# Stage 1 of batches 3 and 4: exponentials, sums and holds in other slots, and the first hi matmul one slot earlier

## The chip, the cores and the metric

The kernel runs on one core of a Trainium2 chip. The metric is the device time of one execution in microseconds (us), as the median of three runs. A core has five engines with an instruction queue each: TensorE (PE in the profile; its weight loads are PEld), VectorE (DVE), ScalarE (ACT), GpSimd (POOL) and SyncE (SP, which issues most DMA transfers here). An engine takes its instructions in order; where one needs another engine's result, it waits for a semaphore, and what is queued behind it waits too. [...]

## The reference, cut to what matters

```python
def mab(q, kv):
    s = scale * (q @ kv.transpose(0, 2, 1))
    s = s - s.max(-1, keepdims=True)
    a = np.exp(s)
    a /= a.sum(-1, keepdims=True) + 1e-09
    return a @ kv

h = mab(I, x)                 # stage 1: 32 learned rows over all 12416 rows of a batch
y = mab(x, h)                 # stage 2: each row of x over the 32 rows of h

gate = 1.0 / (1.0 + np.exp(-(y @ w_gate)))
val = y @ w_val
out = (gate * val @ w_out).astype(np.float32)
```

x has 4 batches of 12416 rows of 128 columns; the gated feed-forward network has 1536 hidden columns.

## The kernel before

**Blocks, steps and slots.** The feed-forward network runs over 97 blocks of 512 rows (24 for each batch and one of the remaining rows). Stage 2's last product is folded into the network: the attention weights `a2r` are multiplied with `hw`, which is h times the network's weights. A block is eight steps, by turns one with two hidden tiles (1024 columns, wide) and one with one (512, narrow). A step is: value matmul into `v_ps`, tanh of the gate on ScalarE (line 971, `t`), the product `u = (t + 1) * v` on VectorE (line 984), and, two steps later, its projection into the accumulator `acc_ps` on TensorE (line 1015). The gate matmul `g_ps` runs two steps ahead. Value and gate banks of each width are single, and so is the accumulator: ScalarE empties it once a block (line 1033, `o`), and the next block's first projection waits for that.

**The order by hand.** Two steps are a slot, a wide product and a narrow one. All work beside the network (stages 1 and 2 of later groups and batches) is written into a table: `at(slot, make, late)` puts a piece at a slot, early behind the wide step or late behind the narrow one. `beside` issues the pieces when their step comes, so the table sets each engine's order. The row tiles of a batch go in groups of 16 (`groups`), six full ones and a small one of one tile, number NG. While the network works on batch b (slots `o` to `o + 95`, with `o = 96 b`, b from 0), stage 1 of batch b + 1 is in the table, and slots given below as plain numbers count from `o`; slots from 100 on count from the start.

**Stage 1.** For a recent group `plan_stage1` puts down: scores on TensorE and their maximum on VectorE (`begin`, lines 217 and 229), the exponential on ScalarE with the negated maximum as its bias (`weigh`, line 242), a transpose by DMA on SP's queue (`turn`, line 266), the sums over x on TensorE in two halves (line 277) and a copy of the sum out of PSUM (`s1_sum_keep`, line 292, `hst`). In batches 3 and 4 (b = 1 and 2 in the loop) this is done for groups 2, 3 and NG alone, with scores at slots 7, 11 and 32. The four older groups, `SHARED`, go by `plan_shared`: their scores are copied to SBUF (line 337), share one maximum that GpSimd works out, and are weighed later (line 374). They are summed in pairs: two groups into one bank, `hp`, and one copy (`hold`, line 386) for each pair. Scores, sums and several other small results use the one PSUM bank with the tag "m", each after the one before has been read. The kept sums are joined at slot 54 (`plan_combine`, `join`).

**Stage 2's first whole group.** The group right after the start is done with `soon`: its maximum is split on GpSimd into two bf16 parts, `hi` and `lo` (lines 546 and 548), which two matmuls with an identity add onto the scores in PSUM (`s2_shift`, line 555); the exponential reads PSUM after that.

## Time and profile before

| | |
|---|---|
| median of 3 runs | 722.02 us (721.89 to 722.83) |
| the profiled execution: its time | 722.04 us |
| the profiled execution: its span, first to last instruction | 720.2 us |
| mean granted TensorE clock | 1.000 of full speed |
| VectorE busy in the span | 97% |
| ScalarE busy | 94% |
| TensorE busy (matmuls are pipelined, so this is not TensorE at its peak) | 90% |
| GpSimd busy | 61% |

In a row of the timeline the first number is the start in us from the span's start, the second the time to the end of the row's last instruction; then come the engine (SPq is SP's DMA queue), the line, the operation, the tiles as out<-in, the shape of the row's first instruction (later ones in the row may have another), and the count. In brackets stand idle time ahead of the row and what ended it. `a1T` and `a1` of the code are `a1T` and `a`, `o32` is `o`, `s1_ps` and `s2_ps` are `s_ps`.

### The profile page before, as it was taken

How to read it: one execution, taken by the hardware profiler on the slowest of the kernel's cores; microseconds unless marked ns; L12 is line 12 of the kernel's file. 1: busy time of each engine (PE TensorE's matmuls, PEld its weight loads, DVE VectorE, ACT ScalarE, POOL GpSimd, SP SyncE). 2: the span in 40 equal slices, each digit the busy share in tenths (PEclk: the TensorE clock that was granted, in tenths of full speed). 3: DMA queues.
4: the chain of work that ended last, by engine and by line, in shares of the span. 5: the costliest groups of instructions: out<-in, count | busy, mean ns of one | idle time of the engine just before them, and what ended most of it. 6: DMA issues, size and time to landing. Idle time of an engine off the chain costs nothing.

```text
span 720.2 us, 21611 instructions
## 1 busy us (share of the span) xinstructions
PE 647.8 (90%) x8478; PEld 392.9 (55%) x8478; DVE 700.7 (97%) x865; ACT 675.0 (94%) x1012; POOL 437.6 (61%) x739
## 2 busy tenths in 40 slices
PE   7989889998998999999998989999989899898887
PEld 4555555555555555655555555555555555555555
DVE  4799999999999999999999999999999999999998
ACT  4699999999999999999999999999999999999996
POOL 4464663877558988558657897486746555535100
PEclk9999999999999999999999999999999999999999
DMA  8879935263593255155485132220232123121211
GB/s 171 171 140 177 180 80 106 74 119 83 112 160 77 65 103 114 52 125 112 90 140 118 55 75 62 59 76 33 74 74 60 46 63 70 47 61 45 62 45 46
DMA packets 116726, 65.21 MB, mean 91 GB/s; under 512 B 99824, under 2 KB 101008, under 8 KB 116624
## 3 DMA queue, kind: packets, MB, share of 16 engines
q1 hardware_dynamic: 111936, 49.81, 31.2%
q0 software_dynamic: 4416, 13.90, 10.8%
q8 instruction: 66, 1.08, 0.6%
q14 instruction: 36, 0.29, 0.2%
q10 hardware_dynamic: 272, 0.13, 0.1%
HBM read 27.80 MB, written 25.43 MB: 74 GB/s over the span
## 4 chain that ended last, share of the span: by engine, by line
DVE 52%; issue 22%; PE 14%; ACT 8%; DMA 2%; DVEq 1%; POOL 0%; ACTq 0%; POOLq 0%
DVE u L984 50%; ACT t L971 7%; PE acc_ps L1015 7%; PE v_ps L952 5%; DMA xn<-in_x_dram 2%; DVEq L984 1%; PE hp_ps L277 1%; DVE nm L229 1%; ACT o L1033 1%; PE g_ps L952 1%; PE s_ps L217 0%; POOL xn L82 0%; ACT a1T L242 0%; ACT hwt L434 0%; ACT sc L565 0%
## 5 line engine op out<-in xcount | busy, mean ns | idle before, releaser
L984 DVE SCALAR_TENSOR_TENSOR u<-t,v_ps 128x512 f16<-128x512 f16 (+1 forms) x778 | 676.1, 942 | 2.7 <-PE g_ps L952 1.4
L971 ACT ACTIVATE t<-g_ps 128x512 f16<-128x512 f32 (+1 forms) x777 | 593.0, 819 | 25.4 <-ACT t L971 13.0
L952 PE MATMUL v_ps<-a2r,hwt 32*128 32x512 f16 (+1 forms) x1188 | 293.5, 371 | 59.6 <-DVE u L984 57.2
L1015 PE MATMUL acc_ps<-wo,u 128*128 128x128 f16 x4656 | 327.4, 220 | 1.5 <-ACT o L1033 1.2
L1015 PEld LDWEIGHTS <-u 128*128 128x128 f16 x4656 | 261.5, 98 | 89.3 <-issue 88.3
L952 PE MATMUL g_ps<-a2r,hwt 32*128 32x512 f16 (+1 forms) x1188 | 296.6, 377 | 0.0
L952 PEld LDWEIGHTS <-hwt 32*128 32x128 f16 x2424 | 92.4, 91 | 192.8 <-issue 147.0
L645 POOL TENSOR_TENSOR a2n<-e,rs 128x2048 f16<-128x2048 f16 (+3 forms) x25 | 86.8, 3474 | 5.3 <-DVE rs L617 3.6
L599 POOL TENSOR_TENSOR sum<-e 128x256 f32<-128x256 f16 (+1 forms) x23 | 15.4, 672 | 116.1 <-ACT e L591 116.1
L623 POOL TENSOR_TENSOR near<-sme,minus 128x16 f32<-128x16 f32 (+1 forms) x22 | 65.2, 2961 | 1.7
L1033 ACT ACTIVATE o<-acc_ps 128x512 f32<-128x512 f32 x96 | 58.2, 606 | 0.0
L575 POOL TENSOR_TENSOR rise<-sc 128x256 f32<-128x256 f32 (+1 forms) x22 | 16.3, 739 | 40.7 <-ACT sc L565 40.6
L576 POOL TENSOR_SCALAR rise<-rise 128x256 f32<-128x256 f32 (+6 forms) x110 | 30.1, 273 | 9.7
L579 POOL TENSOR_TENSOR top<-top,rise 128x128 f32<-128x128 f32 (+3 forms) x88 | 28.3, 322 | 7.3
L599 POOL TENSOR_TENSOR sum<-sum 128x128 f32<-128x128 f32 (+3 forms) x92 | 28.3, 307 | 7.2
L575 POOL TENSOR_TENSOR rise<-top 128x128 f32<-128x128 f32 (+3 forms) x88 | 27.2, 309 | 6.9
L582 POOL TENSOR_TENSOR sc<-sc,top 128x512 f32<-128x512 f32 (+1 forms) x22 | 23.9, 1086 | 1.7
L531 PEld LDWEIGHTS <-xT 128*128 128x128 f16 x388 | 13.0, 96 | 11.5 <-issue 11.1
L82 POOL DMA_DIRECT2D xn<-in_x_dram x25 | 14.7, 595 | 6.5 <-DMA xn<-in_x_dram 5.6
L531 PE MATMUL s_ps<-hT,xT 128*128 128x32 f16 x388 | 18.0, 178 | 0.1
L579 POOL TENSOR_TENSOR top<-sc,rise 128x256 f32<-128x256 f32 (+1 forms) x22 | 16.2, 738 | 1.8
L362 POOL TENSOR_SCALAR xT<-xT,nm 128x512 f32<-128x512 f32 x8 | 15.8, 1990 | 0.2
(141 smaller groups left out, 271.3 us busy)
## 6 DMA issues: line engine op xcount, KB each, us to landing
out_dram<-o SPq DMA_DIRECT2D x96, 256.0 KB, 2.3
xn<-in_x_dram POOLq DMA_DIRECT2D x19, 512.0 KB, 7.4
xn<-in_x_dram POOLq DMA_DIRECT2D x4, 544.0 KB, 6.3
a2r<-a2n SPq DMA_TRANSPOSE x29, 4.5
xn<-in_x_dram POOLq DMA_DIRECT2D x1, 384.0 KB, 14.9
wg<-in_moe_w_gate_dram POOLq DMA_DIRECT2D x1, 384.0 KB, 16.4
wv<-in_moe_w_val_dram POOLq DMA_DIRECT2D x1, 384.0 KB, 16.4
wo<-in_moe_w_out_dram POOLq DMA_DIRECT2D x1, 384.0 KB, 15.9
```

Of the source, the lines that this page charges most:

```text
L531: nc.tensor.matmul(s2[:, j, :], xT[b][:, c + j, :], hT16[b][:], start=(j == 0), stop=whole and j == j1 - 1, skip_group_check=True,)
L575: nc.gpsimd.tensor_tensor(out=r, in0=far, in1=near, op=ALU.subtract)
L576: nc.gpsimd.tensor_scalar(out=r, in0=r, scalar1=BIG, scalar2=0.0, op0=ALU.min, op1=ALU.max)
L579: nc.gpsimd.tensor_tensor(out=top[:, 0:n, 0:w], in0=near, in1=r, op=ALU.add)
L599: nc.gpsimd.tensor_tensor(out=d[:, 0:n, :], in0=src[:, :, 0:w], in1=src[:, :, w : 2 * w], op=ALU.add)
L623: nc.gpsimd.tensor_tensor(out=near[:, 0:n], in0=sme[:, 0:n], in1=minus1[:, 0:n], op=ALU.pow)
L645: eng.tensor_tensor(out=a2n[:, 0:n, :, :], in0=e.unsqueeze(2).to_broadcast((P, n, 4, m)), in1=rs.unsqueeze(2).unsqueeze(3).to_broadcast((P ...
L952: st[what + "end"] = nc.tensor.matmul(pt[:, k, col : col + nb * P], hw[b][r : r + 32, j // 2, :], a2r[r : r + 32, o : o + nb, :].rearrange ...
L971: st["tanh"] = nc.scalar.activation(out=st["t"][:, :, c:e], in_=st["g"][:, :, c:e], func=AF.Tanh, scale=0.5)
L984: u = nc.vector.scalar_tensor_tensor(out=st["u"][:, :, c:e], in0=st["t"][:, :, c:e], scalar=1.0, in1=st["v"][:, :, c:e], op0=ALU.add, op1= ...
L1015: nc.tensor.matmul(acc[0][(i // 2) % len(acc[0])][:, i, :], st["u"][:, k, ts(i, P)], wo16[:, NI * (j % 2) + j // 2, :], start=(j == 0 and ...
L1033: nc.scalar.mul(out=o32[:], in_=acc[0][0][:], mul=0.5)
```

## The change

Five edits, four of them in batches 3 and 4:

- the exponentials of groups 2 and 3 stand in the slot of their maximum, late, and not in the next one; their DMA turns follow one slot sooner too;
- each of the four shared sums is issued in two halves, in two slots running; the second pair starts at slots 49 and 51, before 50 and 52;
- the copy of the first pair's sum moves from slot 43 to 45 (the second stays at 53);
- the sum of the small group and its copy move from slot 45 to 47;
- in stage 2's `soon` group the hi matmul is issued in slot 2, the lo matmul stays in slot 3.

No operation is added or taken away, and each engine has as many instructions as before.

```diff
@@ plan_stage1
         at(score, begin)
-        at(score + 1, weigh, late=full)
-        at(score + 2, turn)
+        soon = full and b > 1
+        at(score + (0 if soon else 1), weigh, late=full)
+        at(score + (1 if soon else 2), turn)
@@ plan_shared
-        def part(i):
-            if i % 2 == 0:
+        def part(i, k0, k1):
+            if i % 2 == 0 and k0 == 0:
                 st["hp"] = ps.tile([P, C + 1], F32, tag="m", name="hp_ps")
-            s1_sum_pe(b, SHARED[i], st[i], st["hp"], 0, 4, i % 2 == 0, i % 2 == 1)
+            s1_sum_pe(b, SHARED[i], st[i], st["hp"], k0, k1, i % 2 == 0, i % 2 == 1)
...
-            at(o + sums[i], lambda i=i: part(i))
+            at(o + sums[i], lambda i=i: part(i, 0, 2))
+            at(o + sums[i] + 1, lambda i=i: part(i, 2, 4))
...
-        for k in range(2):
-            at(o + sums[2 * k + 1] + 1, lambda k=k: hold(k))
+        for k, slot in enumerate(holds):
+            at(o + slot, lambda k=k: hold(k))
@@ plan_stage2
         if soon:
-            at(weigh, lambda: s2_shift(GC, st["s2"], *st["hl"]))
+            for k in range(2):
+                at(weigh - 1 + k, lambda k=k: s2_shift(GC, st["s2"], *st["hl"], which=(k,)))
@@ the table of slots
-        single = (32, (45, 45, 45) if b else (43, 43, 43))
+        single = (32, (47, 47, 47) if b else (43, 43, 43))
...
-                b + 1, o, (-6, 2, 10, 14), (7, 11, 15), 23, (26, 30, 42, 46), (40, 42, 50, 52)
+                (26, 30, 42, 46),
+                (40, 42, 49, 51),
+                (45, 53),
```

(`s2_shift` takes the list `which` and issues only the named ones of its two matmuls.)

Three places show how the queues change. The first is ScalarE's queue around slot 103 (7 from batch 2's start), where batch 3's first recent group is weighed; `t` is the network's tanh, `a1T` the exponential, `o` the accumulator's copy. Before:

```order
L971 ACTIVATE t_4680<-g_ps 128x1024
L971 ACTIVATE t_4697<-g_ps 128x512
L971 ACTIVATE t_4719<-g_ps 128x1024
L971 ACTIVATE t_4728<-g_ps 128x512
L242 ACTIVATE a1T<-s_ps,nm_0_137 128x512
L1033 ACTIVATE o_4744<-acc_ps 128x512
L971 ACTIVATE t_4755<-g_ps 128x1024
```

and after:

```order
L974 ACTIVATE t_4680<-g_ps 128x1024
L974 ACTIVATE t_4697<-g_ps 128x512
L242 ACTIVATE a1T<-s_ps,nm_0_137 128x512
L974 ACTIVATE t_4721<-g_ps 128x1024
L974 ACTIVATE t_4732<-g_ps 128x512
L1036 ACTIVATE o_4746<-acc_ps 128x512
L974 ACTIVATE t_4757<-g_ps 128x1024
```

The exponential passes two tanhs and no longer stands directly ahead of the accumulator's copy.

The second is SP's DMA queue in the same place; `a<-a1T` is the turn of the weighed group, `xT<-xn` a transpose of x for a later score. Before:

```order
L656 DMA_TRANSPOSE a2r<-a2n 128x16x128
L91 DMA_TRANSPOSE xT_3912<-xn_1800 128x16x128
L1035 DMA out_dram<-o_4744 128x512
L266 DMA_TRANSPOSE a_4757<-a1T 128x4x128
L1035 DMA out_dram<-o_4887 128x512
```

and after:

```order
L658 DMA_TRANSPOSE a2r<-a2n 128x16x128
L266 DMA_TRANSPOSE a_4723<-a1T 128x4x128
L91 DMA_TRANSPOSE xT_3912<-xn_1800 128x16x128
L1038 DMA out_dram<-o_4746 128x512
L266 DMA_TRANSPOSE a_4867<-a1T 128x4x128
```

The turn, which needs the exponential, now stands ahead of the transpose of x and of an output store.

The third is TensorE's queue at slots 2 and 3, where the `soon` group is shifted; `g_ps` and `v_ps` are gate and value fills. Before:

```order
L952 MATMUL g_ps<-a2r,hwt 128x512
L555 LDWEIGHTS identb
L555 MATMUL s_ps<-hi,identb 128x512
L555 LDWEIGHTS identb
L555 MATMUL s_ps<-lo,identb 128x512
L952 LDWEIGHTS hwt
L952 MATMUL v_ps<-a2first,hwt 128x256
```

and after, where hi now stands:

```order
L955 MATMUL g_ps<-a2first,hwt 128x256
L557 LDWEIGHTS identb
L557 MATMUL s_ps<-hi,identb 128x512
L955 LDWEIGHTS hwt
L955 MATMUL v_ps<-a2first,hwt 128x256
```

hi now precedes a narrow step's value fills in slot 2; lo keeps its place alone.

More of the change, by code (lines that the diff above doesn't have):

```diff
@@ L322, in plan_stage1, with plan_shared @@
         at(keep, lambda: s1_sum_keep(b, s, st["hp"]))
-    def plan_shared(b, o, takes, tops, least, weighs, sums):
+    def plan_shared(b, o, takes, tops, least, weighs, sums, holds):
         st = {}
@@ L551, in s2_max, with s2_shift @@
         return hi, lo
-    def s2_shift(n, s2, hi, lo):
-        for t_, last in ((hi, False), (lo, True)):
+    def s2_shift(n, s2, hi, lo, which=(0, 1)):
+        for t_, last in [((hi, False), (lo, True))[k] for k in which]:
             nc.tensor.matmul(
@@ L1065 @@
             plan_shared(
-                b + 1, o, (-6, 2, 10, 14), (7, 11, 15), 23, (26, 30, 42, 46), (40, 42, 50, 52)
+                b + 1,
+                o,
+                (-6, 2, 10, 14),
+                (7, 11, 15),
+                23,
+                (26, 30, 42, 46),
+                (40, 42, 49, 51),
+                (45, 53),
             )
```

## The prediction, made before the result was known

> **What bounds the kernel now.** I read the page's busy table first, then its costliest groups, then the timelines of VectorE, ScalarE and TensorE stretch by stretch. From the page:

> ```profile
> span 720.2 us, 21611 instructions
> PE 647.8 (90%) x8478; PEld 392.9 (55%) x8478; DVE 700.7 (97%) x865; ACT 675.0 (94%) x1012; POOL 437.6 (61%) x739
> L984 DVE SCALAR_TENSOR_TENSOR u<-t,v_ps 128x512 f16<-128x512 f16 (+1 forms) x778 | 676.1, 942 | 2.7 <-PE g_ps L952 1.4
> ```

> The gated products of line 984 fill the span: VectorE waits only 2.7 us ahead of them. So the time is what the products take back to back, plus other VectorE work, plus what makes a product late. ScalarE at 94% and TensorE at 90% have little room, so work that lands badly on either delays VectorE. The sum is made against this execution's 722.04 us, which encloses the 720.2 us span and is as good as the median of the runs, 722.02. The measure of "late" is an undisturbed stretch, VectorE's timeline in the last batch (start, length, first shape, count):

> ```profile
> 551.38 42.71 DVE L984 SCALAR_TENSOR_TENSOR u<-t,v_ps 128x1024 f16<-128x1024 f16 x49
> ```

> 49 products, starting and ending with a wide one, are 24 slots and a last product of 1.21: a slot is (42.71 - 1.21) / 24 = 1.729 us. The same timeline where batch 3's stage 1 runs, and batch 4's:

> ```profile
> 215.04 1.21 DVE L984 SCALAR_TENSOR_TENSOR u<-t,v_ps 128x1024 f16<-128x1024 f16 x1
> 216.17 0.68 DVE L229 TENSOR_REDUCE nm<-s_ps 128x1 f32<-128x512 f32 x1
> 216.77 4.13 DVE L984 SCALAR_TENSOR_TENSOR u<-t,v_ps 128x512 f16<-128x512 f16 x5
> 221.28 2.99 DVE L984 SCALAR_TENSOR_TENSOR u<-t,v_ps 128x1024 f16<-128x1024 f16 x3 [0.37 <-PE g_ps L952]
> 224.18 0.68 DVE L229 TENSOR_REDUCE nm<-s_ps 128x1 f32<-128x512 f32 x1
> 229.27 2.99 DVE L984 SCALAR_TENSOR_TENSOR u<-t,v_ps 128x1024 f16<-128x1024 f16 x3 [0.35 <-PE g_ps L952]
> ...
> 385.96 0.68 DVE L229 TENSOR_REDUCE nm<-s_ps 128x1 f32<-128x512 f32 x1
> 391.07 2.99 DVE L984 SCALAR_TENSOR_TENSOR u<-t,v_ps 128x1024 f16<-128x1024 f16 x3 [0.37 <-PE g_ps L952]
> 393.97 0.68 DVE L229 TENSOR_REDUCE nm<-s_ps 128x1 f32<-128x512 f32 x1
> 399.06 15.14 DVE L984 SCALAR_TENSOR_TENSOR u<-t,v_ps 128x1024 f16<-128x1024 f16 x17 [0.35 <-PE g_ps L952]
> ```

> The two maxima of a batch lie four slots apart. Undisturbed that would be 4 x 1.729 plus the maximum's own 0.60 (216.17 to 216.77), 7.52 us; measured are 224.18 - 216.17 = 8.01 and 393.97 - 385.96 = 8.01. Each first exponential thus costs 0.49 us. The second has nearly the same idle gap (0.35 for 0.37), so I take 0.48. Over both batches 1.94 us.

> **Part 1: the four exponentials, one slot sooner.** ScalarE's timeline says what makes them costly (an idle mark tells of the time before the row's first instruction); the last three rows are an undisturbed slot with an output copy, two of ScalarE and VectorE's product:

> ```profile
> 217.31 1.51 ACT L971 ACTIVATE t<-g_ps 128x1024 f16<-128x1024 f32 x2 [0.54 <-PE g_ps L952]
> 218.70 0.69 ACT L242 ACTIVATE a1T<-s_ps,nm 128x512 f16<-128x512 f32 x1
> 219.27 0.61 ACT L1033 ACTIVATE o<-acc_ps 128x512 f32<-128x512 f32 x1
> ...
> 255.20 0.61 ACT L1033 ACTIVATE o<-acc_ps 128x512 f32<-128x512 f32 x1
> 255.67 1.53 ACT L971 ACTIVATE t<-g_ps 128x1024 f16<-128x1024 f32 x2
> 255.49 1.21 DVE L984 SCALAR_TENSOR_TENSOR u<-t,v_ps 128x1024 f16<-128x1024 f16 x1
> ```

> and on TensorE:

> ```profile
> 219.93 0.83 PE L1015 MATMUL acc_ps<-wo,u 128*128 128x128 f16 x12 [0.31 <-ACT o L1033]
> ...
> 255.95 0.84 PE L1015 MATMUL acc_ps<-wo,u 128*128 128x128 f16 x12
> ```

> The exponential (218.70) stands directly ahead of the copy that empties the accumulator. The copy comes late, the projection waits 0.31 us for its one bank, the value and gate fills queue behind the projection, and the product at 221.28 is late. Two slots earlier ScalarE sat idle for 0.54 us ahead of 217.31, because the maximum on VectorE had stretched that slot. The exponential moves there.

> It cannot start before the maximum ends, 216.17 + 0.68 = 216.85; with about 0.06 for the signal (an estimate: the copy ends at 219.27 + 0.61 = 219.88 and the projection that it lets go starts at 219.93) it starts at 216.91. It holds ScalarE 0.57 (218.70 to 219.27), so the next tanh starts near 217.48, not 217.31. That tanh is due only at 216.77 + 0.60 + 1.73 = 219.10, when its product is: hidden. The copy follows the two tanhs. From 217.31 to 218.70, where the exponential stood, is 1.39, so the copy starts at 217.48 + 1.39 = 218.87 and the next tanh at 219.35, 0.25 behind the slot's first product at 219.10. In the undisturbed slot it starts 255.67 - 255.49 = 0.18 behind, so copy and tanh come some 0.07 later than normal. In that slot the projection (255.95 above) starts 0.09 after the copy's signal (255.20 + 0.61 + 0.05 = 255.86), so nearly all of this is swallowed; I leave 0.03 for each exponential. Of the 0.49, idle time is 0.37, the overlap of neighbouring products that a gap also loses 0.08 (216.17 + 0.68 against 216.77), and the other 0.04 belongs to the shared score's copy in the next slot, of which I leave 0.03. Gain of part 1: 1.94 - 4 x 0.06 = **1.70 us**. Bounds: the old gaps stay (0), or all goes (1.94); I stay near the upper one because the idle 0.54 us is measured in the very place.

> [...]

> With each exponential its DMA turn moves on SP's queue, ahead of the last full transpose of x (SP's queue in the timeline, then two rows of the list of DMA issues, whose last number is the median time to landing):

> ```profile
> 214.52 2.54 SPq L91 DMA_TRANSPOSE xT<-xn  x1
> 220.29 1.21 SPq L266 DMA_TRANSPOSE a<-a1T  x1
> ...
> xT<-xn SPq DMA_TRANSPOSE x21, 4.7
> a<-a1T SPq DMA_TRANSPOSE x18, 3.2
> ```

> That transpose of x was issued at 214.52; now it stands behind a turn that waits for the exponential, 216.91 + 0.69 = 217.60, and issues for 1.21, so it starts at about 218.85 and lands near 223.6 by the median of 4.7. The first who needs it is the last shared score, in slot 14 beside the product at 229.27. Covered by over 5 us: nothing. The output store behind it goes later; nobody waits for it, with four output buffers. The turn's own result is used six slots on or more.

> **Part 2: shared sums over two slots each.** VectorE in windows of nine products, with a whole sum in each second slot, then with halves in each slot (the recent groups' sums) and with none:

> ```profile
> 274.19 7.79 DVE L984 SCALAR_TENSOR_TENSOR u<-t,v_ps 128x512 f16<-128x512 f16 x9
> 291.95 7.81 DVE L984 SCALAR_TENSOR_TENSOR u<-t,v_ps 128x512 f16<-128x512 f16 x9
> 444.27 7.79 DVE L984 SCALAR_TENSOR_TENSOR u<-t,v_ps 128x512 f16<-128x512 f16 x9
> 461.82 7.82 DVE L984 SCALAR_TENSOR_TENSOR u<-t,v_ps 128x512 f16<-128x512 f16 x9
> 232.18 7.60 DVE L984 SCALAR_TENSOR_TENSOR u<-t,v_ps 128x512 f16<-128x512 f16 x9
> 246.25 7.59 DVE L984 SCALAR_TENSOR_TENSOR u<-t,v_ps 128x512 f16<-128x512 f16 x9
> ```

> A pair of whole sums costs 0.20, 0.22, 0.20 and 0.23 over 7.59; halves cost 0.01 for four of them. So 0.85 - 4 x 0.01 = **0.81 us**, between 0.43 (if a half cost half a whole) and 0.85. The second pair is summed a slot sooner; a turn lands 3.2 us after issue (median) and the last has four slots, 6.9 us.

> **Part 3: holds.** The first hold moves from slot 43 to 45 and the small group's from 45 to 47, each one copy of about 0.28 us. Other such copies stand in slots 17 and 19, within the 7.60 row, so the new places cost nothing. Their bank is asked for again at slots 47 and 49, after the copies. If that cover went, it would be 0.1 to 0.2 us each.

> **Part 4: first hi matmul.** VectorE, GpSimd, then TensorE around slots 2 and 3:

> ```profile
> 35.43 6.65 DVE L984 SCALAR_TENSOR_TENSOR u<-t,v_ps 128x1024 f16<-128x1024 f16 x7
> 34.97 0.20 POOL L546 CAST hi<-nmx 128x16 bf16<-128x16 f32 x1
> 35.09 0.27 PE L952 MATMUL g_ps<-a2first,hwt 32*128 32x256 f16 x2
> 35.55 0.26 PE L952 MATMUL v_ps<-a2first,hwt 32*128 32x256 f16 x1 [0.19 <-DVE u L984]
> 37.04 0.39 PE L555 MATMUL s_ps<-hi,identb 128*128 128x512 bf16 x1
> 37.27 0.38 PE L555 MATMUL s_ps<-lo,identb 128*128 128x512 bf16 x1
> 37.58 0.28 PE L952 MATMUL v_ps<-a2first,hwt 32*128 32x256 f16 x1
> ```

> Seven products should take 3 x 1.729 + 1.21 = 6.40; they take 6.65. One of the two matmuls holds TensorE 0.23 (37.04 to 37.27). Its new place is the 0.19 us gap ahead of 35.55, and hi is ready at 35.17. So it costs about 0.04 there, hidden as the projection after it has room, and slot 3 gets 0.23 back: **0.23 us**, between -0.1 (hi late for TensorE by that much) and 0.25.

> **Sum.** 1.70 + 0.81 + 0.23 = 2.74; 722.04 - 2.74 = **719.3 us**.

> **Rivals.**
> *Only idle time comes back.* VectorE's marked idle in the changed places is 0.37 + 0.35 + 0.37 + 0.35 = 1.44; the sums and the hi shift show none. Then 720.6. Against it: the nine-product windows are 0.20 longer without an idle mark, as neighbouring records overlap. [...] Chance 0.10.
> *The exponential is late in its new slot too.* If it starts 0.25 us later than I think, each of the four copies and projections lags by as much: 4 x 0.25 gives 720.3. For it: the wait on the maximum is new at that place and no row shows it. Chance 0.13.
> *Slower: the transpose of x lands too late.* It is now tied to the exponential. If it landed over 10 us after issue, the shared score would hold TensorE's queue, fills and all, one us for each us, in both batches. To be 0.2% slower (1.44) it must eat 2.74 + 1.44, so land 12.5 us after issue, against a median of 4.7: 723.5 and more. Chance 0.04.
> *The gain is lost elsewhere*, by collisions of the moved copies or by ScalarE's pauses without a releaser, such as the 0.34 here:

> ```profile
> 423.89 1.51 ACT L971 ACTIVATE t<-g_ps 128x1024 f16<-128x1024 f32 x2 [0.34 <-ACT t L971]
> ```

> falling worse than now; 721.3, chance 0.06.

> **Numbers.** My forecast has 0.67. A measurement of this kernel tells some 0.2% from no change, 720.6 here. Faster takes the forecast, the late exponential and half of the first rival: 0.67 + 0.13 + 0.05 = 0.85; same 0.05 + 0.06 = 0.11; slower 0.04. Range: 718.7 (all upper ends, 1.94 + 0.85 + 0.25, and one pause of 0.3 fewer) to 720.6, which takes in the late exponential and the first rival.

> **What would show it.** Right: the marked gaps before the products after each maximum gone, maxima 7.6 us apart, the exponential some 0.06 after the maximum's end, nine products in 7.60 where sums run, seven in 6.4 at 35.43. Wrong: a projection still waiting for the output copy, a shared score waiting for a DMA, or a fill waiting for GpSimd at 35.

## The result and the profile after

The changed kernel takes 718.91 us in the median of seven runs (718.75 to 721.38) against 721.89 (721.75 to 722.83) for the kernel before in the same series: a ratio of 0.9962, 95% interval 0.995 to 0.9973. Its profiled execution took 718.91 us, 3.13 less than the 722.04 of before, with a span of 717.1 us. Some runs take 1 to 4 us longer; in the profiles of such runs TensorE's granted clock falls for 3 to 7 us (to 0.50 to 0.67 in stretches of it), or the network starts later (first product at 32.34 us instead of 31.08), and where this spoils a median, the text says so.

From the page: the span, the busy times, and the groups of the product and of the projection (busy, mean ns of one, then idle time ahead); the last row is the projection before.

```profile
span 717.1 us, 21610 instructions
PE 646.7 (90%) x8478; PEld 392.2 (55%) x8478; DVE 699.7 (98%) x865; ACT 674.7 (94%) x1012; POOL 438.8 (61%) x739
...
L987 DVE SCALAR_TENSOR_TENSOR u<-t,v_ps 128x512 f16<-128x512 f16 (+1 forms) x778 | 675.0, 942 | 0.8 <-ACT t L974 0.7
L1018 PE MATMUL acc_ps<-wo,u 128*128 128x128 f16 x4656 | 327.5, 220 | 0.0
...
L1015 PE MATMUL acc_ps<-wo,u 128*128 128x128 f16 x4656 | 327.4, 220 | 1.5 <-ACT o L1033 1.2
```

A product takes 942 ns in the mean, as before. VectorE's products wait 0.8 us instead of 2.7, and the projection on TensorE, which waited 1.5 us in all, most of it for the accumulator's copy, waits for nothing. VectorE's 1.9 us of idle time are only a part of the 3.1 us. Most of the rest stands in the products' busy time, 675.0 instead of 676.1 (778 records of 942 ns add up to 733 us in both): where a product was a little late, its record overlapped less with the one before it, without an idle mark, and the time covered by records was longer. So the gain is read from the distances between starts. (By the page there is one instruction fewer than before. Those that compute are the same, but of the semaphore instructions ScalarE has four fewer, VectorE one and SyncE two more; this matters below.) VectorE's timeline around the four maxima (start, length, first shape, count):

```profile
215.98 0.68 DVE L229 TENSOR_REDUCE nm<-s_ps 128x1 f32<-128x512 f32 x1
216.58 7.07 DVE L987 SCALAR_TENSOR_TENSOR u<-t,v_ps 128x512 f16<-128x512 f16 x8
223.57 0.68 DVE L229 TENSOR_REDUCE nm<-s_ps 128x1 f32<-128x512 f32 x1
224.17 12.26 DVE L987 SCALAR_TENSOR_TENSOR u<-t,v_ps 128x512 f16<-128x512 f16 x14
...
384.37 0.68 DVE L229 TENSOR_REDUCE nm<-s_ps 128x1 f32<-128x512 f32 x1
384.97 7.08 DVE L987 SCALAR_TENSOR_TENSOR u<-t,v_ps 128x512 f16<-128x512 f16 x8
391.96 0.68 DVE L229 TENSOR_REDUCE nm<-s_ps 128x1 f32<-128x512 f32 x1
```

Between the two maxima of a batch the eight products are now one row without an idle mark, and the maxima are 7.59 us apart (223.57 - 215.98, and 391.96 - 384.37) instead of 8.01. ScalarE at the first of them, from the narrow tanh's slot on:

```profile
215.01 1.56 ACT L974 ACTIVATE t<-g_ps 128x1024 f16<-128x1024 f32 x2
216.69 0.69 ACT L242 ACTIVATE a1T<-s_ps,nm 128x512 f16<-128x512 f32 x1
217.28 1.50 ACT L974 ACTIVATE t<-g_ps 128x1024 f16<-128x1024 f32 x2
218.66 0.61 ACT L1036 ACTIVATE o<-acc_ps 128x512 f32<-128x512 f32 x1
219.14 3.10 ACT L974 ACTIVATE t<-g_ps 128x1024 f16<-128x1024 f32 x4
```

The exponential starts 0.03 us after the maximum's end (215.98 + 0.68 = 216.66), fills the gap in which ScalarE used to wait, and the copy now stands behind two tanhs. On TensorE the projection follows the fills without a wait:

```profile
219.04 0.38 PE L955 MATMUL g_ps<-a2r,hwt 32*128 32x512 f16 x1
219.36 0.84 PE L1018 MATMUL acc_ps<-wo,u 128*128 128x128 f16 x12
220.17 0.39 PE L955 MATMUL v_ps<-a2r,hwt 32*128 32x512 f16 x2
220.24 0.39 PE L955 MATMUL g_ps<-a2r,hwt 32*128 32x512 f16 x2
```

The last row's gate fill is 0.07 behind the value fill, and the product after it 0.03 us late: what is left of the exponential's cost. The shared sums, in windows of nine products as in the prediction, the seven products around the hi matmul, and the ten products from slot 1 on, after and (last row) before:

```profile
273.18 7.59 DVE L987 SCALAR_TENSOR_TENSOR u<-t,v_ps 128x512 f16<-128x512 f16 x9
290.54 7.62 DVE L987 SCALAR_TENSOR_TENSOR u<-t,v_ps 128x512 f16<-128x512 f16 x9
441.57 7.59 DVE L987 SCALAR_TENSOR_TENSOR u<-t,v_ps 128x512 f16<-128x512 f16 x9
458.93 7.62 DVE L987 SCALAR_TENSOR_TENSOR u<-t,v_ps 128x512 f16<-128x512 f16 x9
...
35.36 6.44 DVE L987 SCALAR_TENSOR_TENSOR u<-t,v_ps 128x1024 f16<-128x1024 f16 x7
...
34.76 8.87 DVE L987 SCALAR_TENSOR_TENSOR u<-t,v_ps 128x512 f16<-128x512 f16 x10
...
34.82 8.98 DVE L984 SCALAR_TENSOR_TENSOR u<-t,v_ps 128x512 f16<-128x512 f16 x10
```

7.79, 7.81, 7.79 and 7.82 became 7.59, 7.62, 7.59 and 7.62; 6.65 became 6.44, and 8.98 became 8.87.

To add this up over the whole run, take for each product how much later the next one starts than behind an undisturbed product of its width (0.598 us for a narrow one, 1.131 for a wide one, the medians; the two products of 256 columns are left out). These excesses, in which the maxima and other work of VectorE stand too, sum to 14.01 us before and 10.96 after, so the products account for 3.05 us of the 3.13. Of the rest, 0.07 is the first product's earlier start (31.08 us instead of 31.14). By place, with slots counted from the start:

| products that were late | before, us | after, us |
|---|---|---|
| two slots behind the four maxima | 1.76 | 0.13 |
| beside the shared sums (8) | 0.78 | 0 |
| slot 3 (hi and lo), then slot 5 | 0.23, 0 | 0, 0.08 |
| behind ScalarE's pauses: slots 141, 220, 221, 246, 273, 356, 357 before; 247, 274, 275, 329, 385 after | 0.83 | 0.35 |

The first three rows give 2.56 us, the fourth 0.48. ScalarE's pauses are short stops (idle marks of 0.21 to 0.50 us in the two traces) that the profile gives no reason for; the experiments come to them. The fourth row was in no term of the prediction's sum.

### The profile page after: what moved, and what is told of

Its sections match the earlier page's. It is cut to its first block, busy times and chain, and to the rows that moved or that the text cites. A ratio compares the mean times of both kernels' runs of the same rounds, so it can differ in the third digit from the quotient of the medians.

```text
span 717.1 us, 21610 instructions
## 1 busy us (share of the span) xinstructions
PE 646.7 (90%) x8478; PEld 392.2 (55%) x8478; DVE 699.7 (98%) x865; ACT 674.7 (94%) x1012; POOL 438.8 (61%) x739
## 4 chain that ended last, share of the span: by engine, by line
DVE 48%; issue 20%; PE 14%; ACT 11%; POOL 4%; DMA 2%; DVEq 1%; ACTq 0%; POOLq 0%
DVE u L987 46%; ACT t L974 10%; PE acc_ps L1018 6%; PE v_ps L955 5%; DMA xn<-in_x_dram 2%; POOL a2n L647 1%; DVE nm L229 1%; PE hp_ps L277 1%; POOL near L625 1%; DVEq L987 1%; POOL rise L577 1%; POOL sum L601 1%; POOL top L581 1%; PE g_ps L955 0%; ACT a1T L242 0%
## 5 line engine op out<-in xcount | busy, mean ns | idle before, releaser
L987 DVE SCALAR_TENSOR_TENSOR u<-t,v_ps 128x512 f16<-128x512 f16 (+1 forms) x778 | 675.0, 942 | 0.8 <-ACT t L974 0.7
```

Source lines behind the costliest of these rows:

```text
L987: u = nc.vector.scalar_tensor_tensor(out=st["u"][:, :, c:e], in0=st["t"][:, :, c:e], scalar=1.0, in1=st["v"][:, :, c:e], op0=ALU.add, op1= ...
```

## The experiments

The first four take the change apart, in one series with the kernel before at 722.14 us (721.75 to 724.3, 29 runs).

**Exponentials alone.** The edit to `plan_stage1` and nothing else:

```diff
-        at(score + 1, weigh, late=full)
-        at(score + 2, turn)
+        soon = full and b > 1
+        at(score + (0 if soon else 1), weigh, late=full)
+        at(score + (1 if soon else 2), turn)
```

> The kernel before with the four exponentials and their turns one slot sooner, and nothing else. Theory (the exponential made the accumulator's copy late, and the slot of the maximum has ScalarE room for it): 1.65 to 1.75 us faster than before, so about 720.2; the maxima of a pair 7.6 us apart, no projection waiting for the copy. Rival (only marked idle time comes back): 1.44 us faster, about 720.5. Rival (the exponential is late in its new slot too): under 1 us faster.

Measured: 719.82 us (719.58 to 720.75, 5 runs), ratio 0.9966, 95% interval in brackets [0.9954, 0.9978]. VectorE's timeline:

```profile
215.92 0.68 DVE L229 TENSOR_REDUCE nm<-s_ps 128x1 f32<-128x512 f32 x1
216.52 7.08 DVE L985 SCALAR_TENSOR_TENSOR u<-t,v_ps 128x512 f16<-128x512 f16 x8
...
273.14 7.79 DVE L985 SCALAR_TENSOR_TENSOR u<-t,v_ps 128x512 f16<-128x512 f16 x9
```

The gaps are gone as in the full change, the sums cost what they did. The excesses fall by 2.20 us, more than the 1.63 behind the maxima. Some 0.5 of the difference is ScalarE's pauses: the late products behind them are those of the changed kernel (247, 274, 275, 329, 385), not those of before.

**Sums and holds alone.** The edits to `plan_shared` and the table:

```diff
+            at(o + sums[i], lambda i=i: part(i, 0, 2))
+            at(o + sums[i] + 1, lambda i=i: part(i, 2, 4))
...
+        single = (32, (47, 47, 47) if b else (43, 43, 43))
...
+                (40, 42, 49, 51), (45, 53)
```

> The kernel before with the shared sums in halves and the holds and the small group's sum in their new slots, and nothing else. Theory (a whole sum overfills TensorE's slot by 0.1 us, a half fits): 0.8 us faster, about 721.1; nine products in 7.60 us where sums run. Rival (only marked idle time comes back; the sums show none): no change, 721.9. If pauses of ScalarE without a releaser also met a hold before, up to 0.3 us more.

Measured: 721.12 us (720.91 to 724.71, 12 runs), ratio 0.9989 [0.9977, 1.0001]. The interval just reaches no change; the trace is clearer. The excesses fall by 0.94: 0.78 beside the sums and 0.16 at slot 141.

**The hi matmul alone.**

```diff
-            at(weigh, lambda: s2_shift(GC, st["s2"], *st["hl"]))
+            for k in range(2):
+                at(weigh - 1 + k, lambda k=k: s2_shift(GC, st["s2"], *st["hl"], which=(k,)))
```

> The kernel before with the first hi matmul in slot 2, and nothing else. Theory (it fits into TensorE's gap there): 0.23 us faster, about 721.7; the seven products at 35.4 in 6.40 us. Rival (only marked idle time comes back): no change. This is near what five rounds can tell, so the profile's rows decide.

Measured: 722.08 us (721.8 to 725.9, 12 runs), ratio 1.0009 [0.9996, 1.0022]: no difference that the time can tell. In VectorE's timeline the ten products take 8.87 us as in the changed kernel, 0.11 less than before; slot 3 is no longer late, slot 5 is, by 0.09.

```profile
34.80 8.87 DVE L985 SCALAR_TENSOR_TENSOR u<-t,v_ps 128x512 f16<-128x512 f16 x10
```

**Halves without the moved holds.** Sums in halves, but at the old slots, with the old holds:

```diff
+            at(o + sums[i], lambda i=i: part(i, 0, 2))
+            at(o + sums[i] + 1, lambda i=i: part(i, 2, 4))
...
                 b + 1, o, (-6, 2, 10, 14), (7, 11, 15), 23, (26, 30, 42, 46), (40, 42, 50, 52)
```

> The kernel before with the shared sums in halves at slots 40 to 43 and 50 to 53, but the holds at 43 and 53 and the small group's sum at 45 as before: a hold now stands in the slot of the last half. Theory (ScalarE reaches the copy a slot's length after the half was issued, so it does not wait): as with the holds moved, 0.8 us faster. Rival (the holds had to move, since the copy waits for the half and holds up the tanh): ScalarE waits for TensorE at the holds, and at least 0.1 us for each of four holds is lost again, so 0.4 us faster or less.

Measured: 721.37 us (721.08 to 722.28, 11 runs), ratio 0.9986 [0.9977, 0.9994]. All eight late products beside the sums are gone here too. What stays is the 0.16 of slot 141, just behind a pause of ScalarE at row 703 of its trace (rows are explained below). With the hold moved, as in the run before, one row fewer stands ahead, the wide tanh there becomes row 702, and the late product is gone; in the run with the exponentials alone it is gone too, with the hold in its old slot. So the hold's place as such was not what cost: moving it shifted the pause.

**Why the old place of the exponential was costly.** The prediction said: because it stood directly ahead of the accumulator's copy. Here it stays in its old slot but goes ahead of the narrow tanh, so a tanh lies between:

```diff
-        at(score + 1, weigh, late=full)
+        at(score + 1, weigh, late=full and b < 2)
```

> The kernel before, with the four exponentials still in the slot after their maximum but early there, behind the wide tanh instead of behind the narrow one: a tanh now stands between each of them and the accumulator's copy. Theory (what counts is ScalarE's work between its last idle time and the copy, which is the same): the copies come as late as before, the gaps of 0.35 to 0.37 us stay, time within 0.2 us of before. Rival (standing directly ahead of the copy is what costs): the gaps go, 1.6 us faster.

Measured: 721.48 us (721.24 to 724.17, 12 runs), against 721.96 (721.75 to 725.55, 29 runs) for the kernel before in this series; ratio 0.9994 [0.9983, 1.0005]. ScalarE's timeline, TensorE's and VectorE's:

```profile
218.23 0.68 ACT L242 ACTIVATE a1T<-s_ps,nm 128x512 f16<-128x512 f32 x1
218.80 0.60 ACT L971 ACTIVATE t<-g_ps 128x512 f16<-128x512 f32 x1
219.28 0.61 ACT L1033 ACTIVATE o<-acc_ps 128x512 f32<-128x512 f32 x1
```

```profile
219.94 0.83 PE L1015 MATMUL acc_ps<-wo,u 128*128 128x128 f16 x12
...
221.28 2.99 DVE L984 SCALAR_TENSOR_TENSOR u<-t,v_ps 128x1024 f16<-128x1024 f16 x3 [0.37 <-PE g_ps L952]
```

The copy starts at 219.28, where it started before (219.27), the projection starts at 219.94 (219.93 before), and the 0.37 us gap stays. So adjacency was not the cause. The exponential's 0.57 us delay the copy at either of the two places between ScalarE's idle 0.54 us and the copy; placed in that idle time, as in the change, it leaves a product 0.03 us late. The 0.5 us by which the median is lower is again the pauses, as far as the trace shows (0.49 of an excess 0.57 smaller): the late products at 141, 220, 221, 246, 273, 356 and 357 are gone, and those at 247, 274, 275, 329 and 385 are there.

**Both shift matmuls in slot 2.**

```diff
-            at(weigh, lambda: s2_shift(GC, st["s2"], *st["hl"]))
+            at(weigh - 1, lambda: s2_shift(GC, st["s2"], *st["hl"]))
```

> The kernel before with both shift matmuls, hi and lo, in slot 2. Theory (TensorE's gap there is 0.19 us wide and each matmul takes 0.23): the second one makes slot 2 late by about 0.2 us, where slot 3 was before, so no gain, the seven products at 35.4 again near 6.6 us. Rival (any place but slot 3 is free): they take 6.4 us, and the time is at or under that with hi alone moved.

Measured: 722.11 us (721.96 to 724.72, 12 runs), ratio 1.0005 [0.9994, 1.0017], so no gain shows. Its profile is of a run whose clock was 0.50 from 33.9 to 37.3 us (the projection at 34.07 takes 1.46 us, the one at 37.44 takes 0.84), so it can't say what lo costs in slot 2; slot 3 is no longer late, and slot 5 is late by 0.10 again.

**Why slot 5 is late.** ScalarE of the changed kernel, then TensorE's fills of slot 5:

```profile
38.51 0.60 ACT L593 ACTIVATE e<-s_ps 128x512 f16<-128x512 f32 x1
38.98 1.53 ACT L974 ACTIVATE t<-g_ps 128x1024 f16<-128x1024 f32 x2
40.36 0.64 ACT L1036 ACTIVATE o<-acc_ps 128x512 f32<-128x512 f32 x1
40.84 2.63 ACT L974 ACTIVATE t<-g_ps 128x1024 f16<-128x1024 f32 x3
```

```profile
41.85 0.39 PE L955 MATMUL v_ps<-a2r,hwt 32*128 32x512 f16 x2
41.97 0.39 PE L955 MATMUL g_ps<-a2r,hwt 32*128 32x512 f16 x2
```

ScalarE runs without a break from the `soon` group's exponential to the wide tanh at 40.84, and the gate fill, which needs that tanh's bank, comes 0.12 behind the value fill. With the exponential cut to 8 of its 16 row tiles (the other 8 are set to 1 by GpSimd, so half of that group's weights are left out):

```diff
+                st["e"] = s2_exp_low(h, st["s2"])
+                nc.gpsimd.memset(st["e"][:, h:n, :], 1.0)
```

> The changed kernel with the exponential of stage 2's first whole group (slot 3, late) over 8 of its 16 row tiles only; the other 8 are set to 1 by GpSimd, so half of that group's weights are left out. Theory: the late product of slot 5 (0.08 us in the changed kernel) comes from ScalarE, which runs without a break from this exponential over two tanhs and the accumulator's copy to the wide tanh that frees the gate bank (the fill at 41.97 us instead of 41.85); with the exponential shorter by 0.15 to 0.25 us the copy and that tanh come earlier by 0.1 or more, the late product falls below 0.03, and nothing else moves: 718.8, which the time alone cannot tell. Rival (stage 2's score matmuls in slots 5 and 6, or the copy of the scores, make it): the late product of 0.08 stays.

Measured: 718.8 us (718.74 to 718.84, 5 runs), ratio 0.995 [0.9936, 0.9964]. ScalarE, TensorE and VectorE:

```profile
38.45 0.39 ACT L593 ACTIVATE e<-s_ps 128x256 f16<-128x256 f32 x1
```

```profile
41.80 0.39 PE L960 MATMUL v_ps<-a2r,hwt 32*128 32x512 f16 x2
41.81 0.39 PE L960 MATMUL g_ps<-a2r,hwt 32*128 32x512 f16 x2
```

```profile
34.68 8.79 DVE L992 SCALAR_TENSOR_TENSOR u<-t,v_ps 128x512 f16<-128x512 f16 x10
```

The exponential is 0.21 shorter, the gate fill no longer lags, and slot 5's product is on time: 8.79 instead of 8.87. The time itself, 718.8 against 718.91, cannot tell 0.08 us. So the stall that the hi matmul made had hidden a second one: while TensorE was late by 0.23, ScalarE's exponential had that much room.

**The same split for batch 2's sums.** On top of the change, two whole sums of batch 2, which make a product late by 0.1 us each at slots 24 and 31, are begun a slot sooner:

```diff
-            early = [(9, (16, 17, 17)), (13, (24, 24, 24))]
-            later = [(25, (31, 31, 31)),
+            early = [(9, (16, 17, 17)), (13, (23, 24, 24))]
+            later = [(25, (30, 31, 31)),
```

> The changed kernel, with the two whole sums of batch 2 (slots 24 and 31, each followed by its copy in the same slot) in halves too, the first half one slot sooner. Theory (a half fits into a slot, a whole costs 0.1 us): the two late products of 0.1 us at 76 and 89 us go, 0.2 us faster than the changed kernel, about 718.7. Rival (the late product there comes from the copy, which stays): no change.

Measured: 721.18 us, scattered (718.79 to 724.22, 12 runs), ratio 0.998 [0.9963, 0.9998]. TensorE at slots 23 and 30:

```profile
73.42 0.24 PE L277 MATMUL hp_ps<-xn,a 128*32 128x128 f16 x4 [0.41 <-ACT sc L567]
...
87.43 0.24 PE L277 MATMUL hp_ps<-xn,a 128*32 128x128 f16 x4 [0.70 <-DMA a<-a1T]
```

The old 0.1 us are gone and larger stalls have come: the first half asks for the bank before ScalarE has copied the scores out of it, and for its turn before the DMA has landed. Then the other way round, with the second half and the copy of the group scored at 25 one slot later (in the version with five added rows, below):

```diff
-            later = [(25, (31, 31, 31)),
+            later = [(25, (31, 32, 32)),
```

> The changed kernel with five copies, and of batch 2 the second half of the sum of the group scored at slot 25, and its copy, moved from slot 31 to 32 (the first half stays at 31, where the DMA turn has landed). Theory (a half sum beside each slot is hidden, and the stalls of the earlier try came from a half that stood ahead of its turn's landing at slot 30 and ahead of the bank's release at slot 23): the 0.10 us late product of slot 31 goes and no new one comes, 0.1 less than with five copies, 718.2 to 718.4, if the rows still miss the wide tanhs. Rival (batch 2's stretch has no room, GpSimd and the DMA queues being late there): a new late product at 32 of 0.1 us or more, and 718.4 to 718.8.

Measured: 719.41 us (719.16 to 720.65, 5 runs), ratio 0.9968 [0.9956, 0.998], about 1 us above the version without this edit. TensorE at slot 32:

```profile
91.34 0.22 PE L220 MATMUL s_ps<-xT,indT 128*32 128x128 f16 x1 [1.07 <-ACT hst L295]
```

The small group's score of slot 32 asks for the bank that the copy, now in that slot too, still holds. The bank's users had been listed for batches 3 and 4 and not for batch 2: both tries failed on that, or on the DMA, so neither says whether TensorE has the room.

**ScalarE's pauses.** The pauses without a releaser stand, in the kernel before, at rows 703, 1087, 1215 and 1727 of ScalarE's trace, counted from 0 with its semaphore instructions, and in the changed kernel at 1215 and 1343: each is 63 more than a multiple of 128. The change takes four semaphore rows off ScalarE (1874 to 1870), so all later rows move against this count. ScalarE of the changed kernel:

```profile
468.53 1.02 ACT L974 ACTIVATE t<-g_ps 128x1024 f16<-128x1024 f32 x1 [0.50 <-ACT t L974]
...
515.69 1.51 ACT L974 ACTIVATE t<-g_ps 128x1024 f16<-128x1024 f32 x2 [0.32 <-ACT t L974]
```

If this is the cause, rows added in the lead-in must move the pauses. The changed kernel with five one-column copies there, a shift by which no such row falls on a wide tanh:

```diff
+    spare = const.tile([P, 1], F16, tag="spare")
+    for _ in range(5):
+        nc.scalar.copy(out=spare[:], in_=idle[:, 0, 0:1])
```

> The changed kernel with five one-column copies on ScalarE ahead of its first work, in the time when it waits for x. They compute nothing that is used. In both profiles each pause of ScalarE without a releaser stands at a row of its queue that is 63 and a multiple of 128, and is seen where that row is a wide tanh. Theory (ScalarE pauses at every 128th row of its queue): five more rows put none of these rows on a wide tanh, so the pauses at 468.5 and 515.7 us and the late products behind them go, 0.3 us faster than the changed kernel, about 718.6. Rival (the pauses belong to points of time or to transfers): they stay at those times and the time does not change.

Measured: 718.38 us (718.16 to 719.88, 6 runs), ratio 0.9946 [0.9929, 0.9963]. No wide tanh has such a number, and the late products at 247, 274, 275 and 329 are gone; slot 385 is back to what it was before the change. Together that is 0.35 us. Four of the six runs lie at 718.16 to 718.42, where six of the changed kernel's seven lie at 718.75 to 718.98. The traces account for about half of this difference: against the 0.35 us stand 0.13, since slots 0 and 1 lose 0.06 and 0.07 to 0.08 us with added copies (read from the runs with seven and 33 copies and from the one with the sum at slot 32), for a reason that no run shows. With seven copies (`range(7)`):

> The changed kernel with seven one-column copies on ScalarE in the lead-in instead of five; nothing else differs. Theory (ScalarE pauses at every 128th row of its queue, and it shows where that row is a wide tanh): counted on the trace of the changed kernel, a shift by seven rows puts such rows on five wide tanhs, a shift by five on none, no shift on four; so the late products of 0.05 to 0.16 us come back at other slots, and the time is 718.8 to 719.2 us, 0.3 to 0.8 above the kernel with five copies (718.38). Rival (the added copies do something else that helps, or the pauses stand at fixed places of the program): the time stays with that of five copies, 718.2 to 718.5.

Measured: 720.24 us (718.72 to 722.63, 12 runs), ratio 0.9972 [0.996, 0.9984]. The median is that of a later start (the profiled run's first product comes at 32.34 us, the changed kernel's at 31.08); the four fastest of the 12 lie at 718.72 to 718.86, 0.4 to 0.6 above the four fastest with five copies. ScalarE:

```profile
138.34 1.51 ACT L977 ACTIVATE t<-g_ps 128x1024 f16<-128x1024 f32 x2 [0.34 <-ACT t L977]
```

This is row 319; rows 447 and 703 are wide tanhs too. The new late products are just behind these three: slots 58 and 59 (0.26), 85 (0.09) and 139 (0.07). The count had named five places. Four are wide tanhs in the trace; the fourth, row 63 at 40.38 us, cost nothing. Last, the kernel before with 33 such rows (27 at the start, six later in the lead-in):

> The kernel before with 33 one-column copies on ScalarE in idle stretches of the lead-in (27 at its start, 6 ahead of the first exponential of stage 2), a shift that by the count on its trace puts no row of number 63 plus a multiple of 128 on a wide tanh. Theory: the pauses at 282, 424, 470 and 661 us and the late products at slots 140, 141, 220, 221, 246, 273, 356 and 357 (0.84 us together; the one at 141 may stay, 0.16) go with nothing else changed, so the time falls by 0.5 to 0.9 to 721.1 to 721.5; the gaps after the maxima, the late products beside the shared sums and slot 3 stay. Rival (the pauses belong to the work at those places): the time stays at 722.0 within 0.2.

Measured: 722.63 us (721.14 to 726.39, 12 runs), ratio 1.0012 [0.9998, 1.0026]. The median tells nothing: in the profiled run (725.08) a sum at slot 31 waits 2.05 us for its DMA turn and the clock falls after it. What the trace does show is that the late products at 141, 220, 221, 246, 273, 356 and 357 are gone, 0.83 us, and that two came at 133 and 321, 0.15, behind rows 703 and 1599, which are wide tanhs after all. The gaps behind the maxima and the sums' 0.1 us stayed. The three fastest runs, 721.14 to 721.53, lie under all 23 of the kernel before in this series (721.9 and up).

## Why the prediction was right, point by point

**The bound.** Right: the time fell by what the products had been late, 3.05 of 3.13 us, with the length of a product unchanged (942 ns).

**Part 1, 1.70 us.** Measured 1.63 (1.76 - 0.13). The step was right: the gaps went, the exponential starts 0.03 after the maximum's end (0.06 was estimated), the copy 2.68 after the maximum's start (218.66 - 215.98; 218.87 - 216.17 = 2.70 was worked out), and 0.03 is left in each of the slots concerned. The reason given was too narrow: "directly ahead of the copy" is not what costs, as the early exponential showed: at the other place tried between ScalarE's idle time and the copy the gap was 0.37 us as well. The exponential held ScalarE 0.59 us here (216.69 to 217.28) where 0.57 had been taken, with no consequence that could be told.

**Part 2, 0.81 us.** Measured 0.79 by the four windows; the halves are as free as those of the recent groups (7.59 and 7.62 us for nine products, against 7.59 and 7.60).

**Part 3, nothing.** Right for the table as it is: the moved copies make nothing late. That moving one of them would also shift a pause and win 0.16 us, as in the run with sums and holds alone, was not seen.

**Part 4, 0.23 us: the mis-sized term.** The step said that slot 3 "gets 0.23 back" and followed it no further than that slot. It did get it back, but 0.11 to 0.15 us is what remains (8.98 to 8.87 by the row, 0.23 less 0.08 by the slots), since, with the stall gone, ScalarE behind its exponential is the next to be late (slot 5). The rule that a stall's removal must be followed to what is late next was applied to the exponentials and not here.

**Rivals.** Only idle time coming back (720.6) fell: the sums' 0.79 came back without an idle mark ahead of a product. VectorE's busy share rose from 97.3% to 97.6% (700.7 of 720.2 us, 699.7 of 717.1), but it counts as work the 1.0 us by which the late products had lengthened the busy time, so it does not show this part of the loss. The exponential was not late in its slot. The transpose of x was issued 2.71 us after the maximum's start (218.69 - 215.98; 2.68 was forecast, 218.85 - 216.17), and nobody waited for it. ScalarE's pauses, named as a way to lose gain, did move, but in the other direction.

**The time.** 2.74 was predicted and 3.13 came. The three terms of the sum gave 2.5 to 2.6 and not 2.74; the other 0.5 is the pauses, for which the sum had no term (the range's lower end alone allowed for one of 0.3 fewer). This part was luck: the prediction did not reckon on which work of ScalarE the pauses would fall. Without it the time would have been about 719.4. And 718.91 lies within the range only by that one pause: the upper ends of the three terms alone (1.94 + 0.85 + 0.25) give 719.0. Taken alone, the edits gain 2.20, 0.94 and 0.12, together more than the 3.05 of the whole, since the first two each shift some of the same pauses.

## What to carry to other kernels

When an engine off the path is idle in one slot and late in the next, move work into the idle time (1.63 us here); between the idle time and the late instruction, the other order tried did not help (its gaps stayed at 0.35 to 0.37 us). After taking a stall away, follow each engine until it next has slack: here the stall of 0.23 us had been slack for another engine, and 0.08 came back. Before splitting work over two slots, list who asks for its bank in both, and when its inputs land. Before crediting an edit with the last few tenths of a us, look whether it moved something that has nothing to do with it, as the pauses here.

## What the runs showed of the hardware

**Pauses at rows a multiple of 128 apart.** In the traces of before, of the change, and of the runs with exponentials alone, the early exponential, seven copies and 33 copies, 23 rows of ScalarE with a number of 63 plus a multiple of 128 are wide tanhs. Of these, 19 start 0.36 to 0.39 us after the end of their gate fill (the other four show no such delay: row 63 with seven copies, and row 1855 in three traces, in which the product of slot 385 is late by 0.06 all the same). Of the wide tanhs with another number that ScalarE waited for, 190 to 199 in each trace, none starts more than 0.13 us after it. Where the number falls on another instruction, no late product was put down to it. One on a wide tanh cost 0.06 to 0.26 us of products (row 63 with seven copies: none), and the kernel with five one-column copies in an idle lead-in, where no such row is a wide tanh, was the fastest of this study, 718.38 us. Where the step of 128 rows comes from, no run here tells.

**The clock fell after a wait of 2 us, and once with no cause in sight.** Granted clock in stretches (the number behind the last bracket of busy times), of the changed kernel with five copies and of the kernel before with 33:

```profile
30.00:34.00 4.00, 3.44 (x49) 1.67 (x49) 3.42 (x7) 3.60 (x6) 2.26 (x3) 1.00 0.50 100
34.00:38.00 4.00, 4.00 (x40) 2.36 (x37) 3.25 (x5) 2.60 (x4) 1.32 (x3) 0.57 0.44 98
```

```profile
88.00:92.00 4.00, 1.95 (x54) 1.24 (x50) 2.26 (x3) 2.06 (x4) 0.00 (x0) 0.98 1.04 215
92.00:96.00 4.00, 4.00 (x30) 2.01 (x27) 2.78 (x4) 2.84 (x4) 0.00 (x0) 0.50 0.35 75
```

In the second case TensorE waits 2.05 us within the first stretch; in the next one the clock is 0.50, and the products from slot 31 to 35 lose 3.9 us in all, more than the wait itself. After the 1.07 us wait at 91 us in the run with the sum at slot 32 the clock stayed at 1.00 (the projections at 91.81 and 93.33 us took 0.84 and 0.83 us, the one at 88.81 before it 0.84). In the first case TensorE had worked as in the changed kernel (3.44 us of the four ahead in both); its clock stayed at 1.00 there and fell to 0.57 here, which cost 1.5 us.
